# A wider first Q load, an early second K load, and the projections of head group 1 moved ahead of the values

## The chip, the cores and the metric

The kernel runs on one core of one Trainium2 chip. The metric is the device time of one execution in microseconds (us). Several executions of each kernel are timed; medians are quoted, and a profile of one execution gives the trace.

Abbreviations: PE is TensorE's matmuls, PEld its weight loads, DVE VectorE, ACT ScalarE, POOL GpSimd, SP SyncE (which issues nearly all DMAs).

## The reference

Two branches of one input x (2048 tokens of 512 values, bf16) are mixed by a gate. Branch A is sliding-window attention with 32 heads of 16 and a window of 256; branch B is a SwiGLU block.

```python
x = A_x
g = sigmoid((x * gate_w).sum(-1, keepdims=True))
# A
q, k, v = split((x @ wqkv))                       # 32 heads of 16
scores = einsum(q, k) * 16 ** -0.5, masked to 0 <= i - j < 256
a = (softmax(scores) @ v) @ wo
# B
b = (silu(x @ w1) * (x @ w3)) @ w2                # hidden size 1376
out = g * a + (1 - g) * b
```

## The kernel before

The heads go in four groups (c = 0 to 3) of 128 channels. For each group and each 512 tokens the kernel projects Q and K (L313), computes scores in "bursts" of 32-row matmuls into the PSUM tile `big` (L684), takes the exponential on ScalarE, masks, and multiplies by V ("pv" groups, L758). The bursts are 76 in all. Between them, the PE is filled with V projections (L360), the matmuls of branch B (L454, L504, L552) and the output projection (L582).

The order on each engine is fixed when the program is built. A small scheduler in Python places operations by assumed durations, by the assumed landing time of each load, and by two numbers: when the first burst is due (T0) and how far apart bursts are due (PACE). Nothing in it is measured at run time; each engine is then given its list in that order.

```python
dma("x0", "SP", 4.1, lambda: x_dma(0, 0))       # name, issuing engine, assumed landing
dma("x1", "SP", 4.8, lambda: x_dma(0, 1))
dma("q0", "SP", 6.4, lambda: w_dma(nc.sync, wq_sb, A_wqkv, 0, P))          # 128 KB
dma("k0", "ACT", 5.8, lambda: w_dma(nc.scalar, wk_sb, A_wqkv, 0, P, D))    # 128 KB
dma("v", "SP", 7.5, lambda: w_dma(nc.sync, wv_sb, A_wqkv, 0, D, 2 * D))    # 512 KB
dma("x2", "SP", 10.2, lambda: [xt_dma(1, c) for c in range(NDC)])          # DMA transposes
...
T0, PACE, NWARM = 12.5, 2.62, 6                  # NWARM: dummy matmuls at the start
...
def fin(eng):                                    # store of one output tile m of 16
    ...
    for i in range(0, n, n // (2 if m < 9 else 1)):
        j = i + n // (2 if m < 9 else 1)
        nc.sync.dma_start(out=out2d[m * P:(m + 1) * P, n0 + i:n0 + j], in_=ot[:, i:j])
```

Output tiles 0 to 8 are stored by two DMAs each, the others by one, and the last tile in three pieces (two from SyncE, one from ScalarE between them).

The softmax here doesn't subtract the row's maximum and nothing guards it: scores larger than these inputs give would overflow.

## Time and profile before

Before the prediction, three runs gave a median of 231.51 us (231.4 to 231.77).

| Reading | Value | View |
|---|---|---|
| span, PE busy | 229.5 us, 220.9 us (96%) | page |
| first useful matmul | 4.13 us (x0 has landed) | timeline |
| first burst, last burst | 12.47 us, 209.88 us | timeline |
| last matmul ends | 226.74 us | timeline |
| distance of bursts | mostly 2.59 to 2.60 us | timeline |

The page's head and its busy line (busy us, share of the span, instructions):

```profile
span 229.5 us, 7237 instructions
PE 220.9 (96%) x3026; PEld 101.6 (44%) x3060; DVE 178.8 (78%) x312; ACT 177.6 (77%) x148; POOL 175.0 (76%) x395
```

The Trainium skill ("Perfetto Trace Analysis", § Identifying the Most-Contended Engine) says that matmul busy time is no good measure of headroom, so the 96% needs a check. The waits view for PE before (engine, what was about to run, what it waited for: total us, times, longest us) has these first lines, and the rest are gaps of 0.2 us, all but one of them put down to "issue":

```profile
PE g_143 L1007 <- DVE scr L106: 1.1, 1, 1.1
PE g_150 L242 <- DMA xs_91<-in_A_x_dram: 0.3, 1, 0.3
PE big L684 <- ACT e_618 L692: 0.2, 1, 0.2
PE g_161 L242 <- DMA xs_93<-in_A_x_dram: 0.2, 1, 0.2
```

Two neighbouring bursts late in the PE timeline before (start us, duration us, line, instruction, count):

```profile
204.69 0.37 PE L684 MATMUL big<-qt_3521,kt_3520 32*128 32x320 bf16 x8
...
207.28 0.31 PE L684 MATMUL big<-qt_3521,kt_3520 32*128 32x320 bf16 x4
```

The two bursts start 2.59 us apart. In that stretch the compiled order has work for 2.35 us, counting a 512-column matmul as 0.213 us and four 32-row matmuls of a burst side by side as one. (The 0.213 is an estimate of the pure column time, half of the 0.427 us between the half-rate dummy matmuls at the start of this trace; at full rate such matmuls start 0.216 us apart.) The 0.24 us left over is what a burst costs on top. Most of it lies where the PE changes its tile shape: at the first burst, the 512-column matmul before it takes 0.31 us (12.16 to 12.47), and the burst takes 0.33 us (12.47 to 12.80) for the columns of 0.213. The same 0.24 to 0.25 us comes out for most intervals, and the others hold a pv group, a group of L504 or a short wait, so between the first and last burst there are almost no gaps to fill.

The head of the PE timeline before, cut (L242 transposes x, L313 projects Q and K, L360 projects V):

```profile
4.13 0.61 PE L242 MATMUL g_150<-on,xs_91 128*128 128x128 bf16 x4 [0.33 <-DMA xs_91<-in_A_x_dram]
...
5.65 0.60 PE L313 MATMUL g_175<-xT,wk_sb 128*128 128x256 bf16 x4
...
6.32 0.38 PE L313 MATMUL g_184<-xT,wq_sb 128*128 128x256 bf16 x2
...
7.41 1.03 PE L360 MATMUL g_199<-e_89,xT 128*128 128x512 bf16 x4
...
12.47 0.40 PE L684 MATMUL big<-qt_174,kt_173 32*128 32x320 bf16 x8
```

The DMA view of the same head before (transfer, issuing queue, size, us from issue to landing). V is the tile `e_89`:

```profile
e_89<-in_A_wqkv_dram SPq DMA_DIRECT2D x1, 512.0 KB, 5.0
wq_sb<-in_A_wqkv_dram SPq DMA_DIRECT2D x1, 128.0 KB, 3.8
```

V is issued at 2.32 us and so lands at 7.3 us, for a first use at 7.41 us. It is just in time in this execution, and a later landing would stall the PE.

### The profile page before, as it was taken

The numbers are of one execution on the slowest core, as the hardware profiler recorded it, in microseconds if no ns is written. First come the engines' busy times: TensorE is split into PE (matmuls) and PEld (weight loads), VectorE is DVE, ScalarE is ACT, GpSimd is POOL, SyncE is SP. The second block draws the span as 40 slices with busy tenths as digits, with TensorE's granted clock in tenths as the row PEclk, the third lists the DMA queues.
The fourth block names the chain that finished last, engine by engine and source line by source line (L and its number), as shares of the span: only waits on it lengthen the run. The fifth ranks groups of instructions, "written<-read, shape, count | busy, mean of one in ns | idle before, by whom it ended". The sixth has DMA issues, their size and how long they took to land.

```text
span 229.5 us, 7237 instructions
## 1 busy us (share of the span) xinstructions
PE 220.9 (96%) x3026; PEld 101.6 (44%) x3060; DVE 178.8 (78%) x312; ACT 177.6 (77%) x148; POOL 175.0 (76%) x395
## 2 busy tenths in 40 slices
PE   7999999999999999999999999999999999999995
PEld 3543443544344443544353435443443444454544
DVE  1578599999999998768758593959987688876754
ACT  3678899889788899787989799987899877977030
POOL 8058887889888898888778887777788878777200
PEclk9999999999999999999999999999999999999999
DMA  6999999300200000000000000000000001220202
GB/s 183 237 231 340 220 254 356 105 0 4 49 3 3 3 0 0 4 3 4 0 3 0 3 3 0 3 3 4 1 3 0 3 4 36 69 83 0 94 3 93
DMA packets 19697, 13.81 MB, mean 60 GB/s; under 512 B 8656, under 2 KB 19376, under 8 KB 19664
## 3 DMA queue, kind: packets, MB, share of 16 engines
q1 hardware_dynamic: 18560, 11.93, 20.3%
q0 software_dynamic: 432, 1.25, 2.7%
q8 instruction: 24, 0.39, 0.7%
q10 hardware_dynamic: 672, 0.16, 0.3%
q14 instruction: 9, 0.07, 0.1%
HBM read 8.55 MB, written 2.10 MB: 46 GB/s over the span
## 4 chain that ended last, share of the span: by engine, by line
PE 92%; issue 2%; DMA 2%; DVE 1%; ACT 1%; SPq 0%; ACTq 0%
PE big L684 11%; DMA xs_93<-in_A_x_dram 2%; PE g_1926 L552 1%; PE g_1432 L552 1%; PE g_3613 L552 1%; PE g_3348 L552 1%; PE g_2183 L552 1%; PE g_4283 L552 1%; PE g_2784 L552 1%; PE g_1655 L552 1%; PE g_4505 L552 1%; PE g_4323 L552 1%; PE g_3014 L552 1%; PE g_4389 L552 1%; PE g_3812 L552 1%
## 5 line engine op out<-in xcount | busy, mean ns | idle before, releaser
L454 PEld LDWEIGHTS <-w_sb 128*128 128x128 bf16 x320 | 29.1, 98 | 35.2 <-issue 4.0
L758 PEld LDWEIGHTS <-Vn 64*32 64x32 bf16 x720 | 15.1, 91 | 3.4 <-issue 1.1
L758 PEld LDWEIGHTS <-Vs 64*32 64x32 bf16 x720 | 15.2, 91 | 0.2
L783 DVE STREAM_TRANSPOSE OT<-on 128x512 bf16<-128x512 bf16 x16 | 11.2, 703 | 0.1
L313 PEld LDWEIGHTS <-wq_sb 128*128 128x128 bf16 x68 | 6.1, 98 | 7.0 <-issue 1.8
L313 PEld LDWEIGHTS <-wk_sb 128*128 128x128 bf16 x68 | 6.1, 98 | 6.9 <-issue 1.1
L360 PEld LDWEIGHTS <-xT 128*128 128x128 bf16 x64 | 5.8, 98 | 7.1 <-issue 1.1
L582 PEld LDWEIGHTS <-OT 128*128 128x128 bf16 x60 | 5.6, 98 | 6.8 <-issue 0.2
L384 POOL DMA_DIRECT2D Vs<-Vn x4 | 2.5, 616 | 5.9 <-ACT Vn L368 5.6
L396 DVE SCALAR_TENSOR_TENSOR OT<-OT 128x512 bf16<-128x512 bf16 x8 | 6.5, 815 | 0.0
L552 PEld LDWEIGHTS <-hT_2300 128*128 128x128 bf16 (+1 forms) x44 | 4.0, 97 | 5.0 <-issue 0.6
L552 PEld LDWEIGHTS <-hT_632 128*128 128x128 bf16 (+1 forms) x44 | 4.0, 98 | 4.7 <-issue 0.4
L552 PEld LDWEIGHTS <-hT_354 128*128 128x128 bf16 (+1 forms) x44 | 4.0, 98 | 4.4 <-issue 0.2
L558 ACT ACTIVATE bsb<-g_4389,omg 128x512 bf16<-128x512 f32 x1 | 0.7, 687 | 6.2 <-PE g_4389 L552 6.2
L552 PEld LDWEIGHTS <-hT_3273 128*128 128x128 bf16 (+1 forms) x33 | 3.1, 98 | 3.8 <-issue 0.2
L708 POOL TENSOR_SCALAR_AFFINE_SELECT e_973<-e_973 64x256 bf16<-64x256 bf16 x6 | 3.7, 614 | 0.4
L708 POOL TENSOR_SCALAR_AFFINE_SELECT e_253<-e_253 64x256 bf16<-64x256 bf16 x6 | 2.5, 411 | 1.9 <-ACT e_253 L692 1.7
L1007 PE MATMUL g_143<-tt_86 128*128 128x512 bf16 x6 | 2.7, 630 | 1.1 <-DVE scr L106 1.1
L708 POOL TENSOR_SCALAR_AFFINE_SELECT e_691<-e_691 64x256 bf16<-64x256 bf16 x6 | 2.8, 466 | 0.9 <-ACT e_691 L692 0.6
L504 PEld LDWEIGHTS <-w_sb 128*32 128x32 bf16 x96 | 2.1, 96 | 3.1 <-issue 1.3
L708 POOL TENSOR_SCALAR_AFFINE_SELECT e_3831<-e_3831 64x256 bf16<-64x256 bf16 x6 | 2.5, 410 | 1.1 <-ACT e_3831 L692 0.8
L708 POOL TENSOR_SCALAR_AFFINE_SELECT e_4113<-e_4113 64x256 bf16<-64x256 bf16 x6 | 2.5, 410 | 1.1 <-ACT e_4113 L692 0.8
(929 smaller groups left out, 848.6 us busy)
## 6 DMA issues: line engine op xcount, KB each, us to landing
w_sb<-in_B_w_dram SPq DMA_DIRECT2D x2, 864.0 KB, 9.3
w_sb<-in_B_w_dram SPq DMA_DIRECT2D x1, 1280.0 KB, 7.2
out_dram<-ot SPq DMA_DIRECT2D x19, 64.0 KB, 1.6
Vs<-Vn POOLq DMA_DIRECT2D x8, 136.0 KB, 4.4
w_sb<-in_B_w_dram SPq DMA_DIRECT2D x2, 512.0 KB, 5.1
OT<-in_A_x_dram SPq DMA_DIRECT2D x1, 1024.0 KB, 10.5
out_dram<-ot SPq DMA_DIRECT2D x6, 128.0 KB, 2.1
e_89<-in_A_wqkv_dram SPq DMA_DIRECT2D x1, 512.0 KB, 5.0
```

What stands on the lines that cost most here:

```text
L313: nc.tensor.matmul(b[:, 0:n], lhsT=(wq_sb if is_q else wk_sb)[:, dc, c * P:(c + 1) * P], rhs=xT[:, dc, t0:t1], start=(dc == 0), stop=(dc = ...
L360: nc.tensor.matmul(b[:], lhsT=xT[:, c, m * P:(m + 1) * P], rhs=wv_sb[:, c, :], start=(c == 0), stop=(c == NDC - 1))
L384: nc.gpsimd.dma_start(out=Vs[0:HK, ms, 0:VW], in_=Vn[HK:P, ms, 0:VW])
L396: nc.vector.scalar_tensor_tensor(out=x, in0=x, scalar=1.0, in1=gw, op0=ALU.mult, op1=ALU.mult, accum_out=zt[:, m:m + 1])
L454: nc.tensor.matmul(b[:], lhsT=wsb[:, dc, f * P:(f + 1) * P], rhs=xT[:, dc, t * 512:(t + 1) * 512], start=(dc == 0), stop=(dc == NDC - 1))
L552: nc.tensor.matmul(b[:], lhsT=h_tile[t][0:fs, f, (m % 4) * P:(m % 4 + 1) * P], rhs=w2_sb[0:fs, f, :], start=(f == 0), stop=(f == NFC - 1))
L582: nc.tensor.matmul(b[:, 0:n], lhsT=OT[:, c * S + m * P:c * S + (m + 1) * P], rhs=wo_t[c // 2][:, c % 2, n0:n1], start=(c == 0), stop=(c == ...
L684: nc.tensor.matmul(big[:, u, col:col + q1 - q0], lhsT=kt[32 * u:32 * u + 32, (j % 8) * P:(j % 8 + 1) * P], rhs=qt[32 * u:32 * u + 32, q0 - ...
L708: nc.gpsimd.affine_select(out=tri, in_=tri, pattern=[[0, 4], [-1 if far else 1, HK]], compare_op=ALU.is_ge, fill=0.0, base=-1 if far else ...
L758: nc.tensor.matmul(pv[i][32 * u:32 * u + 32, a - qa:b - qa], lhsT=v_of(j, i, 4 * c + u), rhs=e_tile[k][i * HK:i * HK + HK, u, col:col + b ...
L783: nc.vector.transpose(out=OT[:, c * S + qa:c * S + qb], in_=st["on"][:, 0:nb].rearrange("p b i d -> p (b i d)"))
L1007: nc.tensor.matmul(b[:], lhsT=warm[:, 0, :], rhs=warm[:].to_broadcast([P, 4, P]), start=(i == 0), stop=(i == NWARM - 1))
```

## The change

Intent: V is the big load that the head waits for. If Q and K of the second head group are loaded ahead of V, the PE has 1.7 us more of useful work before it needs V, and the first burst can come earlier.

```diff
-    dma("x0", "SP", 4.1, lambda: x_dma(0, 0))
+    dma("x0", "SP", 3.8, lambda: x_dma(0, 0))
     dma("x1", "SP", 4.8, lambda: x_dma(0, 1))
-    dma("q0", "SP", 6.4, lambda: w_dma(nc.sync, wq_sb, A_wqkv, 0, P))
-    dma("k0", "ACT", 5.8, lambda: w_dma(nc.scalar, wk_sb, A_wqkv, 0, P, D))
-    dma("v", "SP", 7.5, ...)
-    dma("x2", "SP", 10.2, ...)
+    dma("k0", "ACT", 4.6, lambda: w_dma(nc.scalar, wk_sb, A_wqkv, 0, P, D))
+    dma("q0", "SP", 6.2, lambda: w_dma(nc.sync, wq_sb, A_wqkv, 0, 2 * P))
+    dma("k1", "SP", 7.0, lambda: w_dma(nc.sync, wk_sb, A_wqkv, P, 2 * P, D))
+    dma("v", "SP", 8.5, ...)
+    dma("x2", "SP", 11.2, ...)
     ...                            # assumed landing of wa 13.6 -> 14.4
-    dma("kq", ...)                 # rest of K and Q from column P
+    dma("kq", ...)                 # ... from column 2 * P
@@
-        w = loads[("q0" if is_q else "k0") if c == 0 else "kq"]
+        w = loads[("q0" if is_q else f"k{c}") if c <= 1 else "kq"]
@@
-    T0, PACE, NWARM = 12.5, 2.62, 6
+    T0, PACE, NWARM = 11.5, 2.59, 6
@@
-            for is_q in (False, True):
+            for is_q in ((True, False) if (c, t0) == (1, 0) else (False, True)):
```

The compiled PE order has the same 3060 matmuls before and after. The program has one hardware DMA more (k1).

More of the change, by code (lines that the diff above doesn't have):

```diff
@@ L133 @@
     nc.scalar.activation(out=scr[:, 1:2], in_=scr[:, 0:1], func=ACT.Tanh)
-    dma("x0", "SP", 4.1, lambda: x_dma(0, 0))
+    dma("x0", "SP", 3.8, lambda: x_dma(0, 0))
     dma("x1", "SP", 4.8, lambda: x_dma(0, 1))
-    dma("q0", "SP", 6.4, lambda: w_dma(nc.sync, wq_sb, A_wqkv, 0, P))
-    dma("k0", "ACT", 5.8, lambda: w_dma(nc.scalar, wk_sb, A_wqkv, 0, P, D))
-    dma("v", "SP", 7.5, lambda: w_dma(nc.sync, wv_sb, A_wqkv, 0, D, 2 * D))
-    dma("x2", "SP", 10.2, lambda: [xt_dma(1, c) for c in range(NDC)])
+    dma("k0", "ACT", 4.6, lambda: w_dma(nc.scalar, wk_sb, A_wqkv, 0, P, D))
+    dma("q0", "SP", 6.2, lambda: w_dma(nc.sync, wq_sb, A_wqkv, 0, 2 * P))
+    dma("k1", "SP", 7.0, lambda: w_dma(nc.sync, wk_sb, A_wqkv, P, 2 * P, D))
+    dma("v", "SP", 8.5, lambda: w_dma(nc.sync, wv_sb, A_wqkv, 0, D, 2 * D))
+    dma("x2", "SP", 11.2, lambda: [xt_dma(1, c) for c in range(NDC)])
     FA = 4 * P
-    dma("wa", "SP", 13.6, lambda: (w_dma(nc.sync, w1_sb, B_w1, 0, FA),
+    dma("wa", "SP", 14.4, lambda: (w_dma(nc.sync, w1_sb, B_w1, 0, FA),
                                    w_dma(nc.sync, w3_sb, B_w3, 0, FA)))
@@ L145 @@
                                    w_dma(nc.sync, w3_sb, B_w3, FA, F)))
-    dma("kq", "SP", 27.0, lambda: (w_dma(nc.sync, wk_sb, A_wqkv, P, D, D),
-                                   w_dma(nc.sync, wq_sb, A_wqkv, P, D)))
+    dma("kq", "SP", 27.0, lambda: (w_dma(nc.sync, wk_sb, A_wqkv, 2 * P, D, D),
+                                   w_dma(nc.sync, wq_sb, A_wqkv, 2 * P, D)))
     dma("x6", "SP", 30.0, lambda: [xt_dma(3, c) for c in range(NDC)])
```

## The prediction

> **What bounds the kernel.** The page gives PE 96% busy of a 229.5 us span (DVE 78%, ACT 77%, POOL 76%), at full granted clock. The Trainium skill ("Perfetto Trace Analysis", § Identifying the Most-Contended Engine) warns that matmul busy time is a poor measure, so I checked it: in the PE timeline 512-column matmuls start 0.216 us apart, and between score bursts (groups of 32-row matmuls into `big`) PE takes 2.59 us for 2.35 us of such columns, again and again. The other 0.24 us is the change of tile shape ("issue 0.4" on PEld before L684, 74 times). The waits view for PE holds little else: 1.1 us at the start, 0.3 and 0.2 us for the x tiles, 0.2 us for one exp, some twenty 0.2 us "issue" gaps. From 4.1 us (x0 lands) to 226.7 us (last matmul) PE is an unbroken stream.
>
> **What the change does.** No compute is added or removed: the compiled PE order has the same 3060 matmuls of the same shapes. q0 grows from 128 to 256 KB, a 128 KB k1 goes ahead of V, the late kq shrinks as much. 1.7 us of PE work (Q and K of group 1) moves in front of V, and one V block fewer stands ahead of the first burst, which comes about 0.85 us earlier (12.47 to 11.6). The scheduler's pace is 2.59 instead of 2.62, but PE already runs at 2.59-2.60. From about burst 53 on the compiled order is the same (the last 1102 matmuls).
>
> **Cost in loads.** V lands at 7.3 us and is used at 7.41, just in time; x2's transposes land at 8.8-11 us, used from 10.86. The extra 256 KB and one more SP issue (0.5 us) should delay V and x2 by 0.5-1 us (estimate from 250-300 GB/s in the windows 2-6 us), to about 8.2 and 11.7. But V is now wanted at about 9.1 and x2 at 13.1: both hidden. q0 is tight: landing 5.6 before, perhaps 5.9-6.2 now, first used at 6.2-6.3.
>
> **On the critical path.** There is hardly an idle gap to fill; the sum changes only by transitions. Before: 13 pv groups directly after a burst (0.20 us extra each), two more on their own (0.65 us together), two early groups of 32-column matmuls L504 (0.12 each), one 0.3 us stall for an exp near 30 us. After: 15 pv groups after a burst, none on its own but the last, one L504 group more. Net about -0.3 us if nothing new waits, against perhaps +0.1 for new small waits (q0, an exp or a free PSUM bank).
>
> **Prediction:** 231.25 us, range 230.5 to 231.9. Faster by over 2%: 0.01; within 2%: 0.98; slower by over 2%: 0.01.
>
> **What would show it.** First L684 at about 11.6 us; last burst at 209.6 +- 0.5 and last matmul at 226.4 +- 0.5 (the gain of the head given back by burst 53); PE busy time unchanged within 1 us; V's first matmul at about 9.1 without a DMA wait; burst spacing still 2.59-2.60; the separate pv groups near 41 and 78 us gone.
>
> **What would make it wrong.** PE is in order, so a late landing costs its whole length: q0 after 6.3, or kq and x4 after their first use because one more transfer shifts the queue. A new DMA wait on PE adds to the time. If the gain is over 0.8 us, the head has hidden slack that my stream count does not see.

## More of the kernel before

The tail of the timeline before, the DVE result and the stores that end the program:

```profile
226.11 1.38 SPq L646 DMA_DIRECT2D out_dram<-ot  x2
226.16 0.35 DVE L642 SCALAR_TENSOR_TENSOR ot<-g_4566,omg,bsb 128x128 bf16<-128x128 f32 x1
226.55 0.36 ACTq L646 DMA_DIRECT2D out_dram<-ot  x1
226.78 0.35 DVE L642 SCALAR_TENSOR_TENSOR ot<-g_4581,omg,bsb 128x128 bf16<-128x128 f32 x1 [0.27 <-PE g_4581 L636]
```

The last DVE result is there at 226.78 + 0.35 = 227.13 us; the span then lasts another 2.41 us.

## The result, and the profile after

After: median 231.69 us (231.64 to 232.24, 6 runs). Before, with its runs beside these: 231.47 us (231.2 to 232.48, 6 runs). The ratio is 1.0009 with a 95% interval of 0.9988 to 1.003. Ratios are the mean time of one kernel's fast runs over that of the other's of the same rounds, so they are not quite the ratio of the medians. The time lies inside the predicted range; but it rose by about 0.2 us (not clear of the noise, since the interval holds 1) where a fall of 0.3 us was forecast. Later (e7) the same kernel gave 232.03 us beside 231.61 us before.

The page's head after:

```profile
span 230.0 us, 7240 instructions
PE 221.0 (96%) x3025; PEld 101.7 (44%) x3060; DVE 180.9 (79%) x316; ACT 175.4 (76%) x144; POOL 174.7 (76%) x395
```

The span is 0.5 us longer with PE busy the same. The head of the PE timeline after (lines are numbered one higher):

```profile
3.96 0.59 PE L243 MATMUL g_151<-on,xs_91 128*128 128x128 bf16 x4
...
5.48 0.60 PE L314 MATMUL g_176<-xT,wk_sb 128*128 128x256 bf16 x4
...
6.15 0.38 PE L314 MATMUL g_185<-xT,wq_sb 128*128 128x256 bf16 x2
...
8.97 0.81 PE L361 MATMUL g_214<-e_89,xT 128*128 128x512 bf16 x3
...
11.44 0.40 PE L685 MATMUL big<-qt_175,kt_174 32*128 32x320 bf16 x8
```

The landings after:

```profile
e_89<-in_A_wqkv_dram SPq DMA_DIRECT2D x1, 512.0 KB, 5.6
wq_sb<-in_A_wqkv_dram SPq DMA_DIRECT2D x1, 256.0 KB, 4.2
wk_sb<-in_A_wqkv_dram SPq DMA_DIRECT2D x1, 128.0 KB, 4.8
```

V is issued at 2.87 us, lands at 8.5 and is used at 8.97 without a wait; the slack is 0.5 us. q0 lands at 1.81 + 4.2 = 6.0 us (5.98 in the trace) and is used at 6.15. Of the waits view for PE, only this line and 0.2 to 0.3 us "issue" gaps are left:

```profile
PE g_144 L1008 <- DVE scr L106: 1.1, 1, 1.1
```

So the head did what was predicted: first burst at 11.44 us. The last burst comes at 209.48 us and the last matmul ends at 226.34 us, 0.40 us earlier than before. All of the PE's work is done earlier, and yet the span is longer. The tail after:

```profile
225.71 1.38 SPq L647 DMA_DIRECT2D out_dram<-ot  x2
225.76 0.35 DVE L643 SCALAR_TENSOR_TENSOR ot<-g_4567,omg,bsb 128x128 bf16<-128x128 f32 x1
226.15 0.36 ACTq L647 DMA_DIRECT2D out_dram<-ot  x1
226.38 0.35 DVE L643 SCALAR_TENSOR_TENSOR ot<-g_4582,omg,bsb 128x128 bf16<-128x128 f32 x1 [0.27 <-PE g_4582 L637]
```

Everything here is the tail of before shifted by 0.40 us. The last DVE result is there at 226.73 us; the end of the span comes 3.28 us later, not 2.41. So 0.87 us were lost after the last computation.

What happens there is not in the views of the profile, which leave semaphore instructions out, but the trace holds them. SyncE closes the program by checking one semaphore pair after another in a fixed order. Read out of the two traces (us from the start of the span, and the semaphore checked):

```
before: last store issued at 227.16, signals semaphore 110
  227.55 S118   227.63 S100   227.70 S102   227.77 S105   228.23 S106   228.31 S107
  228.38 S108   228.45 S109   228.62 S110   228.69 S99    228.76 S97 ...  end 229.54

after:  last store issued at 226.76, signals semaphore 100
  227.14 S118   228.22 S100   228.29 S102   228.75 S105   228.83 S106   228.90 S107
  228.97 S108   229.03 S109   229.10 S110   229.16 S99    229.24 S97 ...  end 230.01
```

Semaphores 100, 102 and 105 to 110 are the eight completion semaphores that the program's hardware DMAs take in turn. In the kernel before, the last store falls on the eighth of them (110), which is checked last: while SyncE works through the others, that store is still on its way, and the checks cost nothing. With k1, every later DMA moves on by one, and the last store falls on the first (100). SyncE now stands at that check until 228.22, and all the others still lie ahead of it: steps of about 0.07 us each, and one pause of 0.46 us (between S102 and S105) that was hidden before. From the moment the last store's check passes to the check of S99, it is 228.22 to 229.16 = 0.94 us after, against 228.62 to 228.69 = 0.07 us before. The difference is the 0.87 us.

### The profile page after: what moved, and what is told of

Read it like the earlier page. It is cut to its first block, busy times and chain, and to the rows that moved or that the text cites. A ratio compares the mean times of both kernels' runs of the same rounds, so it can differ in the third digit from the quotient of the medians.

```text
span 230.0 us, 7240 instructions
## 1 busy us (share of the span) xinstructions
PE 221.0 (96%) x3025; PEld 101.7 (44%) x3060; DVE 180.9 (79%) x316; ACT 175.4 (76%) x144; POOL 174.7 (76%) x395
## 4 chain that ended last, share of the span: by engine, by line
PE 96%; issue 2%; DVE 0%
PE big L685 11%; PE g_144 L1008 1%; PE g_1650 L553 1%; PE g_3614 L553 1%; PE g_2293 L553 1%; PE g_3349 L553 1%; PE g_2556 L553 1%; PE g_1928 L553 1%; PE g_3016 L553 1%; PE g_2168 L553 1%; PE g_4284 L553 1%; PE g_4506 L553 1%; PE g_4324 L553 1%; PE g_4390 L553 1%; PE g_3813 L553 1%
## 5 line engine op out<-in xcount | busy, mean ns | idle before, releaser
L709 POOL TENSOR_SCALAR_AFFINE_SELECT e_246<-e_246 64x256 bf16<-64x256 bf16 x6 | 2.5, 411 | 7.7 <-ACT e_246 L693 7.5
L397 DVE SCALAR_TENSOR_TENSOR OT<-OT 128x512 bf16<-128x512 bf16 x8 | 5.9, 758 | 0.0
L709 POOL TENSOR_SCALAR_AFFINE_SELECT e_1530<-e_1530 64x256 bf16<-64x256 bf16 x6 | 3.7, 610 | 0.3
L709 POOL TENSOR_SCALAR_AFFINE_SELECT e_1261<-e_1261 64x256 bf16<-64x256 bf16 x6 | 3.6, 597 | 0.3
L709 POOL TENSOR_SCALAR_AFFINE_SELECT e_976<-e_976 64x256 bf16<-64x256 bf16 x6 | 3.2, 527 | 0.6 <-ACT e_976 L693 0.3
L709 POOL TENSOR_SCALAR_AFFINE_SELECT e_3832<-e_3832 64x256 bf16<-64x256 bf16 x6 | 2.5, 410 | 1.1 <-ACT e_3832 L693 0.9
L709 POOL TENSOR_SCALAR_AFFINE_SELECT e_2774<-e_2774 64x256 bf16<-64x256 bf16 x6 | 2.5, 410 | 1.1 <-ACT e_2774 L693 0.8
L709 POOL TENSOR_SCALAR_AFFINE_SELECT e_1787<-e_1787 64x256 bf16<-64x256 bf16 x6 | 3.1, 512 | 0.3
```

The lines of the kernel that those rows point to most:

```text
L397: nc.vector.scalar_tensor_tensor(out=x, in0=x, scalar=1.0, in1=gw, op0=ALU.mult, op1=ALU.mult, accum_out=zt[:, m:m + 1])
L709: nc.gpsimd.affine_select(out=tri, in_=tri, pattern=[[0, 4], [-1 if far else 1, HK]], compare_op=ALU.is_ge, fill=0.0, base=-1 if far else ...
```

## The experiments

Theory: the change of order and loads moves almost nothing on the PE, and the tail loses 0.87 us to the position of the last store among the eight semaphores. Rival 1: the early loads or the denser head cost the time. Rival 2: the number of output stores costs it. Four kernels ran first, on one chip, beside 11 runs of the kernel before (median 231.52 us, mean 231.61).

### e1: the last store back on the eighth semaphore

```diff
-            for i in range(0, n, n // (2 if m < 9 else 1)):
+            for i in range(0, n, n // (2 if m < 8 else 1)):     # in the kernel after
```

(and the same in the next line). One DMA fewer, among the 24 stores that are issued from 192 us on; the compiled PE order is unchanged.

> The kernel after, with the store of output tile 8 issued as one DMA instead of two (one hardware DMA fewer long before the end, so that the last store of the program uses the eighth completion semaphore again, as in the kernel before, and not the first). Lane theory: the closing sequence of SyncE checks the semaphores in a fixed order, and what it still has to check after the last landing costs about 0.87 us more in the kernel after; so the span falls by about 0.87 us to 229.1, time about 230.8, ratio to before about 0.997. Rival 1 (early loads or the denser head cost the time): no change, about 231.7. Rival 2 (number of output DMAs matters): about 0.1 us at most from one DMA of 25.

Measured: median 231.54 us (230.76 to 231.82), ratio to before 0.9991 (0.9972 to 1.001). The tail was as the theory said: 2.40 us from the last DVE result to the end. But the time fell less than expected, and the span of the profiled run was even 230.1 us, because its first burst came at 12.30 us instead of 11.44 with the same compiled order. So a second thing varies: the head. By the time alone, e1 didn't settle it.

### e2: the kernel before with its last store on the first semaphore

```diff
-            for i in range(0, n, n // (2 if m < 9 else 1)):
+            for i in range(0, n, n // (2 if m < 10 else 1)):    # in the kernel before
```

> The kernel before, with the store of output tile 9 split in two (one hardware DMA more, so that the last store uses the first semaphore). Lane theory: PE timeline unchanged (last matmul 226.7), span 229.54 + 0.87 = 230.4, time about 232.35, ratio about 1.0038. Rival 1: unchanged, ratio 1.000. Rival 2: at most 0.1 us slower.

Measured: median 232.38 us (231.85 to 232.56), ratio 1.0028 (1.001 to 1.0045); tail 3.27 us. The kernel before, with none of the change in it, gets slower by 0.7 us in the mean (232.29 against 231.61) from one split store. Rival 1 can't explain this; rival 2 allowed at most 0.1 us.

### e3: eight stores fewer, the same semaphore

```diff
-            ... (2 if m < 9 else 1) ...
+            ... (2 if m < 1 else 1) ...                          # in the kernel after
```

> The kernel after, with the stores of output tiles 1 to 8 unsplit: eight hardware DMAs fewer, so the last store lands on the same (first) semaphore as in the kernel after. Lane theory: no gain, time about 231.7, the wait after the last landing still about 0.94 us. Rival 2 (number of output DMAs matters): faster by clearly more than e1.

Measured: median 231.88 us (231.4 to 232.15), ratio 1.0007 (0.999 to 1.0024), so no gain over the kernel after, and rival 2 falls. The expectation for the tail was half wrong, though: it was 2.89 us, not 3.28. The checks behind the last store took 228.83 to 229.38 = 0.55 us, because the pause of 0.46 us was no longer among them. In these traces that pause comes one check later for each DMA taken out of SyncE's list: behind the third check in the kernel after, behind the fourth in e1, behind the seventh in e4, and in e3, with eight fewer, behind the eleventh step. In all fourteen traces it lies between the 79th and the 80th SyncE instruction of the program that the trace holds, so what stays fixed is a place in SyncE's list and not a check. In e3 that place is behind the check of S99, and another gap of the same length near the end is gone there: from S99 to the end it is 0.85 us in e3 as in the others. No run shows the cause of the pause.

### e4: the fifth semaphore

```diff
-            ... (2 if m < 9 else 1) ...
+            ... (2 if m < 5 else 1) ...                          # in the kernel after
```

> The kernel after, with the stores of output tiles 5 to 8 unsplit: four DMAs fewer, last store on the fifth semaphore. Lane theory: after the last landing SyncE has 3 checks of 0.07 us more than with the eighth, so about 0.2 us above e1: span 229.3, time about 231.0. Rival 1: about 231.7. Rival 2: between e1 and e3.

Measured: median 231.7 us (231.3 to 232.28), tail 3.03 us. The expected 0.2 us over e1 was 0.63 us, since here the moving pause fell behind the last store's check. The position of the last store sets how many checks are left; whether the pause is among them counts as much.

### What the heads show

Ahead of the second batch I believed that the landing of q0 explained the varying head. A closer reading of the starts shows two causes. In e1, no DMA held the PE up (waits view); the PE was simply slow. The PE timeline of e1:

```profile
5.70 1.47 PE L314 MATMUL g<-xT,wk_sb 128*128 128x256 bf16 x6
6.98 0.41 PE L314 MATMUL g<-xT,wq_sb 128*128 128x256 bf16 x2
```

Six matmuls of 256 columns take 6.98 - 5.70 = 1.28 us, or 0.213 us each, about twice the 0.112 us of the kernel after at the same place (5.48 to 6.15 with six, 0.67 us in all). The page's clock doesn't show it; the windows view of e1 (us, busy of PE, PEld, DVE, ACT, POOL, then granted clock, DMA share, GB/s) has 1.00:

```profile
6.00:7.00 1.00, 1.00 (x7) 0.69 (x6) 0.20 (x1) 0.53 (x1) 0.31 (x2) 1.00 1.08 366
```

The 1.00 only means that the trace has no clock record for this stretch: the views fill such stretches with full clock. Ten of the fourteen traces hold a record of full clock, and it begins where the distances change, at 5.19 us in the kernel after and at 9.39 us in e13; e1, e5, e8 and e11 hold none. In all fourteen traces the dummy matmuls at the start run at half rate (512 columns in 0.43 us), and the full rate begins at a different moment: from before 3.95 us (e8) over 5.2 us (after) and 7.0 us (e1) to 9.4 us (e13). The Trainium skill ("TensorE: Matmul & The Clock Gate", Part 1: The HAM clock gate) describes this: the array runs at half clock until a window of sustained activity has passed, and the window is free-running, so it doesn't start with the kernel. The traces agree on the two rates and on the variation. The slow rate isn't all of e1's late head, though: q0 landed at 6.71 us there and was used at 6.98, so a fast PE would have stood waiting until 6.75 (in e7 and e8 Q began 0.04 us after the landing). Of the 0.83 us by which Q began later than in the kernel after, only about 0.2 us is the rate's alone. The clean case is e13 (below), where q0 had been there for 1.5 us when Q began.

The other cause is a late load. In e8 (below), the clock was up early, and the PE waited for q0:

```profile
5.24 0.83 PE L314 MATMUL g<-xT,wk_sb 128*128 128x256 bf16 x6
7.21 0.39 PE L314 MATMUL g<-xT,wq_sb 128*128 128x256 bf16 x2 [1.14 <-DMA wq_sb<-in_A_wqkv_dram]
```

### e7 and e8: the kernel after with and without the semaphore, on one chip

The four kernels of this second batch ran beside 11 runs of the kernel before (median 231.61 us, mean 231.69). e7 is the kernel after unchanged; e8 is e1 again.

> The kernel after, unchanged, on the same chip as the three runs beside it. New reading from the first four runs: the first score burst of the same compute order fell anywhere from 11.36 to 12.30 us, and the first Q matmuls began when q0 landed (issue to landing 4.0 to 4.9 us). So a run's time should be a head that is drawn anew each time, plus a tail that the semaphore of the last store sets. Expected: last DVE result to end of span 3.28 us again; first burst between 11.3 and 12.4; median 231.7 +- 0.3.

> The same kernel as e1 (kernel after, last store on the eighth semaphore), now beside the kernel after on one chip. Lane theory: last DVE result to end of span 2.40 us as in e1 and the kernel before, against 3.28 in the kernel after; so mean time below that of the kernel after by 0.6 to 1.0 us over six runs each. Rival (the lane only moves the wait, the head decides): difference below 0.2 us.

Measured: e7 median 232.03 us (231.59 to 232.62), tail 3.27 us. e8 median 231.08 us (230.68 to 232.04), tail 2.40 us. The means are 232.09 and 231.20 us, a difference of 0.89 us where the traces say 0.87. With six runs each the standard error of that difference is about 0.27 us, so that the two agree so closely is luck; that there is a loss of this order is not. e7's median is 0.03 us above the expected range. With e2 and the tails in the traces this settles the theory of the tail.

### e9: q0 from ScalarE

```diff
-    nc.scalar.activation(...Tanh)                 # at the top, loads the table
-    dma("q0", "SP", 6.2, lambda: w_dma(nc.sync, wq_sb, A_wqkv, 0, 2 * P))
+    dma("q0", "ACT", 6.2, lambda: w_dma(nc.scalar, wq_sb, A_wqkv, 0, 2 * P))
+    nc.scalar.activation(...Tanh)                 # in e8, the rest as there
```

> e8 with q0 issued by ScalarE behind k0 at about 1.3 us, not by SyncE behind x0 and x1 at 1.8 us (the table load moves behind it); k1, V and the transposes are issued 0.5 us earlier. Theory that the landing of q0 sets the start of the head: q0 lands 0.3 to 0.5 us earlier, first Q matmul at 6.1-6.4, first burst at or below 11.5 and hardly varying; median 0.2 to 0.4 us below e8. Rival ([...]an earlier issue only takes bandwidth from x1): x1 lands as much later, no gain.

Measured: median 230.85 us (230.71 to 230.99), ratio 0.9964 (0.995 to 0.9978); q0 landed at 1.3 + 4.3 = 5.6 us and Q began at 6.03 us. That looked like success, so e13 repeated it.

### e5: the scheduler's two numbers alone

```diff
-    T0, PACE, NWARM = 12.5, 2.62, 6
+    T0, PACE, NWARM = 11.5, 2.59, 6               # in the kernel before
```

> The kernel before with only the scheduler's two numbers changed (first burst 11.5 instead of 12.5, pace 2.59 instead of 2.62), loads as before. PE-stream theory: first burst at about 11.4-12.0, but the PE sum is the same within 0.1 us (counted transitions 22.2 us against 22.2), last store on the eighth semaphore as before: ratio to before 1.000 +- 0.001. If an earlier first burst were worth anything by itself it would gain up to 1 us.

Measured: median 232.49 us (232.15 to 232.74), ratio 1.0035 (1.0018 to 1.0051): slower by 0.8 us in the mean, and my expectation of no difference was wrong. First burst at 11.61 us, but between first and last burst the PE took 23.19 us above its column count, against 22.25 us after. The waits view for PE has:

```profile
PE g L454 <- DVE kt L328: 0.5, 2, 0.2
PE g L360 <- DMA e<-in_A_wqkv_dram: 0.4, 1, 0.4
PE big L684 <- ACT e L692: 0.2, 1, 0.2
```

The denser early order, without the loads that go with it, waits for V in the head (0.4 us) and for DVE at 34 us and at 162 us (0.23 us each); the wait for ACT at 32 us is in the kernel before, too. The two DVE waits are half of the 0.94 us between first and last burst; the rest I have not located. Counting tile changes in the compiled order doesn't see such waits.

### e10 to e13: a third chip

The last batch ran beside 11 runs of before (median 231.53 us, mean 231.58).

e10 is the kernel before with its narrow q0 issued by ScalarE, as in e9.

```diff
-    dma("q0", "SP", 6.4, lambda: w_dma(nc.sync, wq_sb, A_wqkv, 0, P))
+    dma("q0", "ACT", 6.4, lambda: w_dma(nc.scalar, wq_sb, A_wqkv, 0, P))    # behind k0
```

> The kernel before with its narrow q0 issued by ScalarE behind k0 instead of by SyncE behind the x tiles (V and the transposes move up 0.5 us); compute order and last semaphore as before. If the q0 landing is what the head waits for in both kernels, and V is tight in the kernel before, then the small head stalls (0.2 us for q0, 0.2-0.4 us for V in some executions) go: median 231.0 to 231.3, spread under 0.4 us. What the change of order itself is worth is then the difference to e13: by the transition count 0.22 us plus what V still waits for here.

Measured: median 231.74 us (231.3 to 231.84, 5 runs), ratio 1.0007 (0.9994 to 1.002). No gain, and the expected 231.0 to 231.3 us was missed. Issued 0.5 us sooner, q0 landed no sooner in this trace (5.57 us, 5.58 before); x1 landed at 5.26 us (5.14 before), and the PE waited 0.34 us for it.

e13 is e9 again.

> e9 again, beside e10 on one chip: median 230.85 +- 0.15, spread under 0.4 us, ratio to before about 0.9965; faster than e10 by 0.2 to 0.5 us.

Measured: median 231.28 us (231.06 to 233.21), ratio 1.0003 (0.9978 to 1.0029). The profiled execution was the slow one of 233.21 us. Its PE timeline:

```profile
5.62 1.03 PE L243 MATMUL g<-on,xs 128*128 128x128 bf16 x8 [0.66 <-DMA xs<-in_A_x_dram]
6.45 1.49 PE L314 MATMUL g<-xT,wk_sb 128*128 128x256 bf16 x6
7.72 0.63 PE L314 MATMUL g<-xT,wq_sb 128*128 128x256 bf16 x2
```

The PE waited 0.66 us for x1, and then ran at half rate until 9.4 us; the first burst came at 13.83 us. The Trainium skill ("DMA: Bandwidth & Descriptors", § Issuing engines are not separate DMA queues) says that DMAs run on the same 16 engines whoever issues them. That fits what e10 and e13 show: an earlier issue of q0 was no earlier landing (in e13 it landed at 6.18 us, against 5.98 in the kernel after), and x1 landed later (5.57 us, against 4.86). Whether the wait for x1 also held the clock back in this execution isn't shown. The other five runs of e13 have a mean of 231.32 us, 0.26 us below before, where e9 was 0.83 us below. So the gain of e9 was not repeated, and issuing q0 from ScalarE stays unproven.

e12 undoes the wider Q load alone: q0 narrow, a second narrow q1 behind it, then k1 and V.

```diff
-    dma("q0", "SP", 6.2, lambda: w_dma(nc.sync, wq_sb, A_wqkv, 0, 2 * P))
+    dma("q0", "SP", 6.2, lambda: w_dma(nc.sync, wq_sb, A_wqkv, 0, P))
+    dma("q1", "SP", 6.2, lambda: w_dma(nc.sync, wq_sb, A_wqkv, P, 2 * P))
...
-            ... (2 if m < 9 else 1) ...
+            ... (2 if m < 7 else 1) ...           # last store on the eighth semaphore
```

> The kernel after with the wider first Q load undone: q0 narrow as before, the second narrow Q load behind it, then k1 and V; two output tiles fewer split, so that the last store is again on the eighth semaphore. Compute order as in e1. If the width of q0 is what makes its landing late: q0 lands 0.2 to 0.4 us earlier than in e8 and the first Q matmul waits less; median 230.9 to 231.2. If it is its place behind x0 and x1[...]: landing as in e8 (4.0-5.3 us), median as e8, 231.1 to 231.5, or worse for the extra SyncE issue (0.5 us) ahead of V.

Measured: median 231.31 us (230.79 to 232.0), ratio 0.999 (0.9975 to 1.0005), as e1 and e8 within the spread. In the one profile Q did not wait and V did (0.4 us on the weight loads). So the width of q0 matters too little to show in the time here.

e11 undoes the scheduler's numbers alone.

```diff
-    T0, PACE, NWARM = 11.5, 2.59, 6
+    T0, PACE, NWARM = 12.5, 2.62, 6               # in e1
```

> e1 (kernel after, last store on the eighth semaphore) with the scheduler's two numbers as in the kernel before (12.5 and 2.62). The loads alone. Transition count 22.1 us, the same as after; one more V block ahead of the first burst (about 12.3-13.2 us). PE-stream theory: time as e1 and e8 within 0.3 us, about 231.0 to 231.6. If the new pace is what pays, slower than e8 by more than 0.3.

Measured: median 231.69 us (231.28 to 232.29), ratio 1.0006 (0.9992 to 1.0021). Its mean is 231.70 us, against 231.31 us for e12 on the same chip. My expectation named a difference over 0.3 us as the sign that the pace pays, but with six runs each the standard error is about 0.22 us, so the times alone don't show it. The trace points the same way, 23.65 us above the column count instead of 22.25; it is that of the slowest of the six runs (232.29 us), though. One of the new waits, in a pv group (the profile doesn't name what released it):

```profile
43.67 0.28 PE L759 MATMUL g<-e,Vn 64*32 64x256 bf16 x1 [0.58 <-issue]
```

So the new loads and the new numbers seem to belong together: in its one trace, each alone waits more on the PE. By time this is shown for e5 only.

### All traces in one table

Where the compiled PE order is that of before or of after, the span is a sum of four parts. The third, last burst to last DVE result, was 17.25 us in all of these but e1 (17.40), so it is left out.

| Trace | PE order | first burst | first to last burst | last DVE result to end | last store on |
|---|---|---|---|---|---|
| before | before | 12.47 | 197.41 | 2.41 | eighth |
| e2 | before | 13.08 | 197.17 | 3.27 | first |
| e10 | before | 12.76 | 197.18 | 2.41 | eighth |
| after | after | 11.44 | 198.04 | 3.28 | first |
| e7 | after | 11.57 | 198.04 | 3.27 | first |
| e3 | after | 12.06 | 198.03 | 2.89 | first |
| e4 | after | 11.36 | 198.03 | 3.03 | fifth |
| e1 | after | 12.30 | 198.02 | 2.40 | eighth |
| e8 | after | 12.51 | 198.04 | 2.40 | eighth |
| e9 | after | 11.31 | 198.04 | 2.40 | eighth |
| e12 | after | 11.70 | 198.03 | 2.39 | eighth |
| e13 | after | 13.83 | 198.02 | 2.39 | eighth |

The middle is the same to 0.02 us in nine traces of the order after, on different chips. The order before takes 197.17 to 197.18 us, 0.86 us less, and has 0.85 us less to do there (one V block, four matmuls of 512 columns, stands ahead of its first burst). So the reordering is worth 0.0 us between the bursts. The one trace that I had before the prediction, 197.41 us, holds a stall of 0.24 us near 42 us that the two others lack.

## Why the prediction was right, and where it was wrong

The total was right: 231.69 us in a range of 230.5 to 231.9, "within 2%" at 0.98. Part of that was luck: the sum lacked a cost of 0.87 us, which is more than the 0.65 us between the forecast and the top of its range, and the median stayed inside only because a few tenths were gained elsewhere, which the last paragraph of this section leaves open. Point by point:

- **PE is an unbroken stream, so the gain of the head is given back.** Right. The first burst came at 11.44 us (predicted 11.6), the last at 209.48 (209.6), the last matmul ended at 226.34 (226.4), PE busy moved by 0.1 us, bursts stayed 2.59 to 2.60 us apart, and V was used at 8.97 us (9.1) without a wait.
- **V and x2 hidden, q0 tight.** Right. In the profiled run q0 landed 0.17 us ahead of its use (5.98 and 6.15). In other executions of the same loads the PE waited for it: 0.2 us (e7) and 1.14 us (e8). The order before is exposed to V instead: e2 waited 0.2 us and e5, which has its loads, 0.4 us for V. The change swaps one tight load for another.
- **"Net about -0.3 us" from transitions.** The term was mis-sized: it is 0.0 us by the table. "Two more on their own (0.65 us together)" was the error. In e2 and e10 a separate pv group costs the same 0.2 us as one behind a burst; 0.24 us of my figure was a stall that happened in that one trace. The 0.3 us exp stall did go, but the additional L504 group and another short wait took its place.
- **"There is hardly an idle gap to fill; the sum changes only by transitions."** This step failed, because the sum stopped at the last matmul. The end of the span has its own critical path, and one more DMA at the start moved the last store onto the semaphore that is checked first. That cost 0.87 us (3.28 against 2.41 us), seen in the traces of after, e7 and e2, and undone in e1 and e8.
- **"The head has hidden slack that my stream count does not see."** I named it as a risk for a large gain only. The head in fact varies by 1 us and more between executions, by the moment when the PE reaches full rate and by landings. My count treated one execution's head as the head.

By the traces, +0.87 us at the end and 0.0 in the middle should have made the kernel after slower by 0.87 us; the mean of its 12 runs is 231.97 us, the mean of the 33 runs of before 231.63 us, so only 0.34 us. Put the other way, the 18 runs of e1, e8 and e12 (order after, eighth semaphore) have a mean of 231.32 us, 0.31 us below before. These means pool several chips, and the intervals of e1 and e12 alone include 1. A head that no longer waits for V would explain a gain of that size, but first bursts scatter too much to show it, so this last part stays open.

The version to keep is e8, the kernel after with the store of tile 8 unsplit: ratio 0.9979 (0.9959 to 0.9999) in its own call, 0.9991 in the call of e1. It is under the kernel before in both, though the first interval only just excludes 1 and the second doesn't. Against the kernel after on the same chip it gains 0.89 us.

## What to carry to other kernels

When a change adds or removes a DMA anywhere, look at the end of the trace too, from the last computed result to the end of the span: which completion semaphore the last store signals, and how many checks SyncE still has after it. Take an interval that is repeatable (here first to last burst, 0.02 us over nine traces) to price a reordering, and don't price it from a single trace, in which one chance stall of 0.24 us can look like a cost of the pattern. Assumed landing times and due times that a schedule is built on belong to the loads they were tuned with: in one trace each, either half of this change alone put 0.9 us (e5) and 1.4 us (e11) of new waits into the PE's order.

## What the Trainium skill lacked or had wrong

- No page that I read says that the program's closing sequence on SyncE checks the DMA completion semaphores in a fixed order, so that the last store is cheapest on the one checked last. It belongs beside "Runtime: NRT & Kernel Launch", The ~15µs preamble/postamble breakdown, whose table has the barriers and resets behind a kernel but not these checks. Numbers: 2.39 to 2.41 us from the last result to the end on the eighth semaphore, 3.27 to 3.28 us on the first, 0.87 us between them (2.89 us in e3, where the pause below had moved behind these checks); each check about 0.07 us.
- Nor does a page have the pause of 0.46 us in SyncE's closing checks, which comes one check later for each DMA taken out of SyncE's list (behind the third check in the kernel after, the fourth in e1, the seventh in e4; always between the 79th and the 80th SyncE instruction of the program in the trace). Its cause is open.
- "TensorE: Matmul & The Clock Gate", Part 1, puts the change of rate at around 4 us of sustained matmuls with ±500 ns from run to run; a note on the same page has 6, 11 or 14 slow matmuls for one kernel, which is a wider spread. Here the full rate began anywhere from before 3.95 to 9.4 us, that is from under 2.9 to 8.3 us after the first dummy matmul at 1.06 us, so ±500 ns is too narrow. Between e1 and the kernel after the first burst of the same order moved by 0.86 us with no new DMA wait (a late q0 would have cost most of it at full rate, too); in e13 it came 2.39 us later than in the kernel after, 0.66 us of it a wait for x1. That is 0.4% and 1.0% of the span, about the page's "<1% of a typical kernel span", and yet each is more than the gain that was forecast. The views' granted clock read 1.00 through the slow stretch; the distance of starts (0.213 against 0.112 us for 256 columns) and, in ten traces, the start of the trace's clock record show it.
